# Seven products inside each of seven: a second level of Strassen's scheme in the second feed-forward layer of six groups

## The chip, the cores and the metric

The kernel runs on one core of one Trainium2 chip. The metric is the device time of one execution in microseconds (us); the figure for the kernel before is the median of three runs, 1125.85 us, with runs from 1123.66 to 1127.17. Each core has TensorE (matrix products, in the profile PE; its weight loads PEld), VectorE (DVE), ScalarE (ACT) and GpSimd (POOL) for elementwise work, and SyncE (SP), which issues the transfers. SBUF is the on-chip memory of 128 partitions, PSUM holds the sums that TensorE makes, and DRAM is off the chip.

## The reference

A linear attention is followed by a Fourier mixing of tokens and columns, a normalization, and two feed-forward layers with a residual, all in fp32. Cut to what matters:

```python
# attention on (batch 8, heads 8, seq 576, head_dim 64): softmax of q over head_dim, of k over seq
kv = np.einsum('bhsd,bhse->bhde', k_s, v)
x = np.einsum('bhsd,bhde->bhse', q_s, kv)          # turned to (8, 576, 512)
# mixing and feed-forward
X = np.fft.fft(np.fft.fft(x, axis=1), axis=2)
u = x + np.real(X)
mu = np.mean(u, axis=-1, keepdims=True)
var = np.mean((u - mu) ** 2, axis=-1, keepdims=True)
un = (u - mu) / np.sqrt(var + 1e-06)
ch = np.maximum(un @ w_ch1, 0.0) @ w_ch2           # w_ch1 512 x 2048, w_ch2 2048 x 512
return u + ch
```

## The kernel before

The 8 x 576 tokens are nine groups of 512: eight are made of 512 tokens of one batch each, and one of the 64 that each batch leaves over. The first group uses plain products while the weights arrive. The other eight, numbered by `at` from 1 to 8, use Strassen's seven-product scheme (in Winograd's form) once in each layer: a product of 2 x 2 blocks is made of seven block products instead of eight, at the price of sums of blocks before and after. The sums of the weights' blocks are made once on the chip, put in DRAM (`w1s`, `w2s`) and streamed back for each group through a ring of four SBUF buffers of 1 MB (`load`, `used`). For h, the output of the first layer, the sums are made by GpSimd (`a_side`). `ORDER` is the order of the seven products; `A_AT` and `B_AT` say in which of seven slots the left and the right operand of each product stand. Slots 0, 1 and 3 and, at first, 2 hold raw blocks of h; slots 2, 4, 5 and 6 hold sums after `a_side`. Two matmuls that share one PSUM bank (`ba`, `bb`, `bc`) leave 128 x 512 results.

In `down`, the second layer, each product is 16 matmuls of 128 x 128 weights with 256 columns. While TensorE goes through them, the attention, transform and normalization of the next groups are merged between them as side steps (`merged(down, two + norm)`). The functions that the change touches, empty lines left out:

```python
A_AT = {1: 0, 2: 1, 3: 6, 4: 3, 5: 4, 6: 5, 7: 2}
B_AT = {1: 0, 2: 2, 3: 3, 4: 6, 5: 4, 6: 5, 7: 1}
WA_AT = {1: 0, 2: 1, 3: 6, 4: 2, 5: 4, 6: 5, 7: 3}
WB_AT = {1: 0, 2: 1, 3: 2, 4: 6, 5: 4, 6: 5, 7: 3}
WORDS_AT = [*range(8), 8, 9, 10, *range(3, 8), 0, 1, 2, 8, 9, 10, 4, 5, 6, 7, 8, 11, 12, 7, 13, 8]
LATE_WORDS = (27, 28, 30)
ORDER = (1, 6, 5, 7, 2, 4, 3)
# ... (cut)
    def a_side(self, at, to, e1, e2):
        e1.tensor_tensor(out=to(4), in0=at(2), in1=at(3), op=ALU.add)
        e1.tensor_tensor(out=to(2), in0=at(0), in1=at(2), op=ALU.subtract)
        e2.tensor_tensor(out=to(5), in0=to(4), in1=at(0), op=ALU.subtract)
        e2.tensor_tensor(out=to(6), in0=at(1), in1=to(5), op=ALU.subtract)
# ... (cut)
    def load(self, n):
        g, i = divmod(n, NP + 7)
        if g > B:
            return
        k = n % 4
        w = self.big[:, k * NP * HD:(k + 1) * NP * HD].rearrange("p (a n) -> p a n", n=HD)
        if i < NP:
            self.nc.sync.dma_start(w[:, 0:7, :], self.w1s[i][:])
        else:
            self.nc.sync.dma_start(w, self.w2s[WB_AT[ORDER[i - NP]]])
        self.stream[n] = w
    def hpairs(self, p, n):
        a = 2 * NF * D + p * 7 * HD if p < NP // 2 else NF * D + (p - NP // 2) * 7 * HD
        return self.big[:, a:a + n * 7 * HD].rearrange("p (a s n) -> p a s n", s=7, n=HD)
# ... (cut)
    def strassen(self, product, out, early=lambda *a: None):
        nc, V = self.nc, self.nc.vector
        box = {}
        def bank(n):
            box[n] = self.ps.tile([P, 2, HD], F32, tag=n, name=n)
        def temp(n):
            box[n] = self.work.tile([P, 2, HD], F32, tag=n, name=n, bufs=1)
            return box[n][:]
        def m1():
            nc.scalar.copy(temp("s1"), box["ba"][:])
            early(2, 1, box["s1"])
        def m6():
            V.tensor_tensor(out=temp("u2"), in0=box["bb"][:], in1=box["s1"][:], op=ALU.add)
            early(1, 2, box["u2"])
        def m7():
            V.tensor_tensor(out=temp("u3"), in0=box["bb"][:], in1=box["s1"][:], op=ALU.add)
            early(2, 2, box["u3"])
            out[2, 2](box["bc"], box["u3"])
        ends = {1: m1, 6: m6, 7: m7, 2: lambda: out[1, 1](box["ba"], None),
                4: lambda: out[2, 1](box["bb"], box["s1"]), 3: lambda: out[1, 2](box["bc"], box["u2"])}
        at = {1: "ba", 2: "ba", 6: "bb", 7: "bb", 4: "bb", 5: "bc", 3: "bc"}
        steps = []
        for m in ORDER:
            first = m in (1, 6, 5)
            parts = product(m, lambda m=m: box[at[m]], first, m in (2, 4, 3))
            begin = [lambda m=m: bank(at[m])] if first else []
            end = [ends[m]] if m in ends else []
            steps.append(begin + parts + end)
        return steps
    def up(self, at, unT):
        nc, V = self.nc, self.nc.vector
        steps = []
        for j in range(NP // 2):
            pairs = (2 * j, 2 * j + 1)
            hp = lambda i, h=self.hpairs(2 * j, 2): h[:, :, i, :]
            def product(m, bank, first, last, pairs=pairs):
                def run(i):
                    w = self.stream[15 * at + pairs[i]]
                    for k in range(2):
                        nc.tensor.matmul(bank()[:, i, :], lhsT=w[:, WA_AT[m], k * P:(k + 1) * P],
                                         rhs=unT[:, B_AT[m], k, :], start=first and i == 0 and k == 0,
                                         stop=k == 1,
                                         skip_group_check=True)
                return [lambda i=i: run(i) for i in range(2)]
            def c11(bank, _, hp=hp):
                nc.scalar.activation(hp(0), bank[:], ACT.Relu)
            def other(i, hp=hp):
                def run(bank, u):
                    V.tensor_tensor(out=hp(i), in0=bank[:], in1=u[:], op=ALU.add)
                    nc.scalar.activation(hp(i), hp(i), ACT.Relu)
                    if i == 2:
                        self.a_side(hp, hp, nc.gpsimd, nc.gpsimd)
                return run
            job = self.strassen(product, {(1, 1): c11, (2, 1): other(1), (2, 2): other(3), (1, 2): other(2)})
            steps.append([s for m in job for s in m] + [lambda p=p: self.used(15 * at + p) for p in pairs])
        return steps
    def used(self, n):
        self.stream.pop(n)
        self.load(n + 4)
    def down(self, g, at):
        nc, V = self.nc, self.nc.vector
        h = [self.hpairs(p, 1)[:, 0] for p in range(NP)]
        last = at == B
        def product(m, bank, first, final):
            n = 15 * at + NP + ORDER.index(m)
            order = (1, 0) if last and m == 3 else (0, 1)
            def run(i, q):
                w = self.stream[n]
                for p in range(4 * q, 4 * q + 4):
                    nc.tensor.matmul(bank()[:, i, :], lhsT=h[p][:, A_AT[m], i * P:(i + 1) * P], rhs=w[:, p, :],
                                     start=first and i == 0 and p == 0, stop=p == NP - 1,
                                     skip_group_check=True)
                if (i, q) == (order[1], 1):
                    self.used(n)
                if last and m in (4, 3) and q == 1:
                    sums(m == 4, m != 4, bank(), i)
            return [lambda i=i, q=q: run(i, q) for i in order for q in range(2)]
        def early(i, j, t):
            u, d = i - 1 if (i, j) != (1, 2) else 0, j - 1
            x = self.xs[g, u][:, :, d * HD:(d + 1) * HD]
            nc.gpsimd.tensor_tensor(out=x, in0=x, in1=t[:], op=ALU.add)
        def sums(u, d, bank, i):
            x = self.xs[g, u][:, i, d * HD:(d + 1) * HD]
            V.tensor_tensor(out=x, in0=bank[:, i, :], in1=x, op=ALU.add)
# ... (cut: out, which adds the four results from PSUM into x with VectorE, L1020)
# ... (cut)
        jobs, down = blk.up(order, nexts.pop(g)), blk.down(g, order)
        merged(flat(jobs), one)
        merged(down, two + (norm(groups[order + 1]) if order < B else []))
```

The instructions of these helpers stand in the profile under these lines: L957 is the matmul of `up`, L995 that of `down`; L362 to L365 are `a_side`; L369 to L372 are `b_side` on the normalized input; L921, L925 and L929 are `m1`, `m6` and `m7` of `strassen`; L964, L968 and L969 finish h; L1007 and L1020 add into x. L418 and L420 are the loads of the stream.

## Time and profile before

| what | value |
|---|---|
| time, median of three | 1125.85 us (1123.66 to 1127.17) |
| span of the profiled execution | 1126.2 us |
| mean granted TensorE clock | 0.991 |
| moved by DMA | 193.79 MB, mean 172 GB/s |
| first layers of the groups 1 to 8 (L957), stretch of one | 60 to 63 us (48 to 50 in the last two) |
| second layers of the groups 1 to 8 (L995), stretch of one | 57 to 61 us (49 in the last two) |

How to read it: a row of the groups gives the line, the engine, the operation, the tiles out<-in with their shapes, the count, then busy time in us and the mean duration of one in ns, then the engine's idle time just before these instructions and what ended it. A matmul in fp32 is recorded as two instructions, so the counts of L957 and L995 are twice the number of matmuls in the code. A timeline row gives the start and the length of a run of like instructions in us. A stretch row gives, for a window of time, the busy time and count of each engine.

### The profile page before, as it was taken

How to read it: one execution, taken by the hardware profiler on the slowest of the kernel's cores; microseconds unless marked ns; L12 is line 12 of the kernel's file. 1: busy time of each engine (PE TensorE's matmuls, PEld its weight loads, DVE VectorE, ACT ScalarE, POOL GpSimd, SP SyncE). 2: the span in 40 equal slices, each digit the busy share in tenths (PEclk: the TensorE clock that was granted, in tenths of full speed). 3: DMA queues.
4: the chain of work that ended last, by engine and by line, in shares of the span. 5: the costliest groups of instructions: out<-in, count | busy, mean ns of one | idle time of the engine just before them, and what ended most of it. 6: DMA issues, size and time to landing. Idle time of an engine off the chain costs nothing.

```text
span 1126.2 us, 14461 instructions
## 1 busy us (share of the span) xinstructions
PE 1088.4 (97%) x5376; PEld 909.9 (81%) x5376; DVE 545.4 (48%) x1121; ACT 403.5 (36%) x973; POOL 331.9 (29%) x303
## 2 busy tenths in 40 slices
PE   5789989999999999999999999999999999999997
PEld 4644545887888888898889888888889888888886
DVE  6694796368423734375344643583444352103301
ACT  6695434255233513362325332542334152201200
POOL 1065571235013510324024402251034203402320
PEclk8899999999999999999999999999999999999999
DMA  9555786464246534554356435642453444434451
GB/s 305 176 190 188 259 291 220 145 224 166 98 150 211 195 127 145 195 172 171 125 173 221 150 106 190 198 185 108 147 191 150 144 144 144 187 141 157 152 187 56
DMA packets 92581, 193.79 MB, mean 172 GB/s; under 512 B 23120, under 2 KB 59728, under 8 KB 85344
## 3 DMA queue, kind: packets, MB, share of 16 engines
q1 hardware_dynamic: 90712, 191.82, 49.9%
q10 hardware_dynamic: 1800, 1.05, 0.3%
q8 instruction: 43, 0.70, 0.2%
q14 instruction: 26, 0.21, 0.1%
HBM read 168.72 MB, written 28.31 MB: 175 GB/s over the span
## 4 chain that ended last, share of the span: by engine, by line
PE 81%; POOL 3%; issue 2%; ACT 1%; DVE 1%; ACTq 0%; POOLq 0%
PE bb L957 14%; PE bb L995 14%; PE bc L995 10%; PE ba L957 9%; PE bc L957 9%; PE ba L995 9%; PE acc L568 2%; PE acc L658 2%; PE bc L896 2%; PE acc L752 1%; PE acc L776 1%; PE acc L755 1%; PE tr L857 1%; PE tr L554 1%; PE tr L623 1%
## 5 line engine op out<-in xcount | busy, mean ns | idle before, releaser
L957 PE MATMUL bb<-unT,big 128*128 128x256 f32 x768 | 187.4, 381 | 0.2 <-DVE u L925 0.2
L995 PE MATMUL bb<-big 128*128 128x256 f32 x768 | 172.1, 379 | 0.0
L957 PEld LDWEIGHTS bb<-unT,big 128*128 128x128 f32 x768 | 142.8, 190 | 23.9 <-DVE u L925 3.0
L995 PEld LDWEIGHTS bb<-big 128*128 128x128 f32 x768 | 145.4, 190 | 20.3
L362 POOL TENSOR_TENSOR big<-big 128x512 f32<-128x512 f32 (+1 forms) x38 | 46.2, 1216 | 307.6 <-ACT big L969 306.8
L969 ACT ACTIVATE big<-big 128x512 f32<-128x512 f32 x96 | 60.3, 629 | 182.7 <-DVE big L968 182.2
L957 PE MATMUL bc<-unT,big 128*128 128x256 f32 x512 | 125.4, 379 | 0.0
L957 PE MATMUL ba<-unT,big 128*128 128x256 f32 x512 | 123.6, 379 | 0.2 <-ACT unT L861 0.2
L995 PE MATMUL bc<-big 128*128 128x256 f32 x512 | 116.0, 379 | 0.5 <-DVE x L1012 0.5
L995 PE MATMUL ba<-big 128*128 128x256 f32 x512 | 114.8, 379 | 0.0
L929 DVE TENSOR_TENSOR u<-bb,s 128x512 f32<-128x512 f32 x40 | 27.6, 691 | 173.1 <-PE bb L995 116.1
L995 PEld LDWEIGHTS bc<-big 128*128 128x128 f32 x512 | 96.1, 190 | 14.3 <-DVE x L1012 0.9
L995 PEld LDWEIGHTS ba<-big 128*128 128x128 f32 x512 | 95.7, 190 | 12.1
L957 PEld LDWEIGHTS bc<-unT,big 128*128 128x128 f32 x512 | 95.1, 190 | 12.6
L957 PEld LDWEIGHTS ba<-unT,big 128*128 128x128 f32 x512 | 95.1, 190 | 12.2 <-ACT unT L861 0.5
L370 POOL TENSOR_TENSOR unT<-unT 128x512 f32<-128x512 f32 x8 | 14.2, 1772 | 179.8 <-DVE unT L369 179.8
L607 ACT ACTIVATE q<-q,qm 128x64 f32<-128x64 f32 x240 | 61.6, 338 | 6.8 <-DVE qm L605 6.6
L925 DVE TENSOR_TENSOR u<-bb,s 128x512 f32<-128x512 f32 x40 | 27.5, 688 | 71.7 <-PE bb L957 38.7
L968 DVE TENSOR_TENSOR big<-bc,u 128x512 f32<-128x512 f32 x64 | 44.1, 689 | 22.8 <-PE bc L957 21.7
L1007 POOL TENSOR_TENSOR x<-x,u 128x512 f32<-128x512 f32 x14 | 17.7, 1267 | 118.8 <-DVE u L929 99.0
L861 ACT COPY unT<-tr 128x512 f32<-128x512 f32 x36 | 20.7, 585 | 79.9 <-PE tr L857 79.3
L968 DVE TENSOR_TENSOR big<-bb,s 128x512 f32<-128x512 f32 x32 | 22.1, 691 | 56.1 <-PE bb L957 56.1
(254 smaller groups left out, 1640.8 us busy)
## 6 DMA issues: line engine op xcount, KB each, us to landing
big<-w1s SPq DMA_DIRECT2D x64, 896.0 KB
big<-w2s SPq DMA_DIRECT2D x56, 1024.0 KB
big<-in_w_dram SPq DMA_DIRECT2D x21, 512.0 KB
q<-in_q_dram SPq DMA_DIRECT2D x27, 256.0 KB
k<-in_kT_dram SPq DMA_DIRECT2D x24, 288.0 KB
v<-in_v_dram SPq DMA_DIRECT2D x24, 256.0 KB
words<-in_w_dram SPq DMA_DIRECT2D x8, 512.0 KB
mirror<-x SPq DMA_DIRECT2D x14, 256.0 KB
```

Of the source, the lines that this page charges most:

```text
L362: e1.tensor_tensor(out=to(4), in0=at(2), in1=at(3), op=ALU.add)
L568: nc.tensor.matmul(pk, lhsT=ks[:, c, :], rhs=v[:, c, :], start=(c == 0), stop=(c == NC - 1))
L607: nc.scalar.activation(heads[:, h, :], heads[:, h, :], ACT.Exp, bias=m[:, h:h + 1])
L658: nc.tensor.matmul(px[:, r * P:(r + 1) * P], lhsT=qT[:, r, :], rhs=self.kvr[b % 2][:, r, :], start=True, stop=True)
L861: nc.scalar.copy(unT[:, u:u + 3:2, :, cols], pt[:].rearrange("p (a k) t -> p a k t", a=2))
L896: nc.tensor.matmul(po[:], lhsT=h[:, f, i * P:(i + 1) * P], rhs=self.w2sb[:, f, :], start=(f == 0), stop=(f == NF - 1))
L925: V.tensor_tensor(out=temp("u2"), in0=box["bb"][:], in1=box["s1"][:], op=ALU.add)
L929: V.tensor_tensor(out=temp("u3"), in0=box["bb"][:], in1=box["s1"][:], op=ALU.add)
L957: nc.tensor.matmul(bank()[:, i, :], lhsT=w[:, WA_AT[m], k * P:(k + 1) * P], rhs=unT[:, B_AT[m], k, :], start=first and i == 0 and k == 0, ...
L968: V.tensor_tensor(out=hp(i), in0=bank[:], in1=u[:], op=ALU.add)
L969: nc.scalar.activation(hp(i), hp(i), ACT.Relu)
L995: nc.tensor.matmul(bank()[:, i, :], lhsT=h[p][:, A_AT[m], i * P:(i + 1) * P], rhs=w[:, p, :], start=first and i == 0 and p == 0, stop=p == ...
```

## The change

The second layer of the groups 2 to 7 (`deep`) is made in two levels of the same scheme: each of the seven block products is itself split into 2 x 2 blocks and made of seven smaller ones. A first-level product had 16 matmuls of 256 columns; now its seven parts have four matmuls of 128 columns each, 28 in all, over half the columns. It is meant to cut the multiplications of this layer by one eighth.

For this the weights need second-level sums. They do not change from group to group, so group 1, which still uses one level, makes them as its first-level sums pass through (`deepen`: two operations on VectorE and two on GpSimd for each product), and writes all 49 weight blocks to DRAM (`w2d`). The deep groups stream `w2d` in place of `w2s`, four blocks (1 MB) per buffer.

The second-level sums of h are made in each deep group (`a_steps`: for each first-level product two on VectorE and two on GpSimd). The seven first-level products are done in four units, `UNITS`: product 1 alone, then three pairs; the two of a pair share the PSUM banks and the evacuations. Within a unit the 14 or 7 small products go in `ORDER`, and the sums for the next unit are spread between them. The result of a first-level product is put together in its own dead slot 0 block and then added into x by GpSimd (`into`), where the scheme before added three results with GpSimd and four from PSUM with VectorE. Because the second level needs the first half and the second half of h's columns apart, `up` now handles the pairs of blocks j and j + 4 together (`PAIRS`).

The core of the diff, empty lines left out:

```diff
+UNITS = ((1,), (2, 4), (7, 6), (5, 3))
+DEEP = [(m, n) for unit in UNITS for n in ORDER for m in unit]
+PAIRS = [(j + NP // 2, j) for j in range(NP // 2)]
...
+        self.plan, self.base = [], {}
+        for at in range(1, B + 1):
+            self.base[at] = len(self.plan)
+            self.plan += [self.w1s[p][:].rearrange("p a n -> p (a n)") for pair in PAIRS for p in pair]
+            if self.deep(at):
+                for i in range(0, len(DEEP), 4):
+                    self.plan.append(self.w2d[:, i:min(i + 4, len(DEEP)), :].rearrange("p a n -> p (a n)"))
+            else:
+                self.plan += [self.w2s[WB_AT[m]].rearrange("p a n -> p (a n)") for m in ORDER]
         self.big = c.tile([P, 3 * NF * D], F32, name="big")
...
+    def deep(self, at):
+        return 1 < at < B
...
+    def deepen(self, m, w, t):
+        nc = self.nc
+        at = lambda i: w[:, i // 2 * 4:i // 2 * 4 + 4, i % 2 * P:i % 2 * P + P]
+        to = lambda i: t[(1, 4, 5, 6).index(i)]
+        e1, e2 = nc.vector, nc.gpsimd
+        e1.tensor_tensor(out=to(4), in0=at(1), in1=at(0), op=ALU.subtract)
+        e1.tensor_tensor(out=to(1), in0=at(3), in1=at(1), op=ALU.subtract)
+        e2.tensor_tensor(out=to(5), in0=at(3), in1=to(4), op=ALU.subtract)
+        e2.tensor_tensor(out=to(6), in0=at(2), in1=to(5), op=ALU.subtract)
+        for n in (1, 2, 3, 5, 7, 6, 4):
+            i = B_AT[n]
+            to_dram = self.w2d[:, DEEP.index((m, n)), :].rearrange("p (f n) -> p f n", n=P)
+            nc.sync.dma_start(to_dram, to(i) if i in (1, 4, 5, 6) else at(i))
+    def deep_down(self, g, at, unT):
+        nc, V, G = self.nc, self.nc.vector, self.nc.gpsimd
+        base = self.base[at] + NP
+        un = lambda i: unT[:, i].rearrange("p k n -> p (k n)").rearrange("p (f n) -> p f n", n=P)
+        dead = lambda m: [self.hblock(A_AT[m], a, b) for a, b in ((0, 1), (1, 0), (1, 1))]
+        temps = {1: [self.gap(i) for i in range(3)], 4: [un(i) for i in range(3)], 2: [un(i) for i in range(3, 6)],
+                 6: dead(1), 7: [self.gap(i) for i in range(3)], 5: dead(4), 3: dead(2)}
+        result = {m: self.hblock(A_AT[m], 0, 0) for m in A_AT}
+        tile = lambda m: result[m].rearrange("p (c e) n -> p c e n", c=2)
+        def own(m):
+            def at(i):
+                return temps[m][i - 4] if i > 3 else self.hblock(A_AT[m], i // 2, i % 2)
+            return at
+        def a_steps(unit):
+            steps = []
+            for m in unit:
+                to = own(m)
+                for o, x, y, e, op in ((4, 2, 3, V, ALU.add), (2, 0, 2, V, ALU.subtract), (5, 4, 0, G, ALU.subtract),
+                                       (6, 1, 5, G, ALU.subtract)):
+                    steps.append(lambda to=to, o=o, x=x, y=y, e=e, op=op: e.tensor_tensor(out=to(o), in0=to(x), in1=to(y),
+                                                                                          op=op))
+            return steps
+        def into(u, d, m):
+            x = self.xs[g, u][:, :, d * HD:(d + 1) * HD].rearrange("p c (e n) -> p c e n", n=P)
+            G.tensor_tensor(out=x, in0=x, in1=tile(m), op=ALU.add)
...
+        after = {(1,): [lambda: into(0, 0, 1)],
+                 (2, 4): [lambda: into(1, 0, 4), lambda: into(0, 0, 2)],
+                 (7, 6): [lambda: sums(6, 1), lambda: into(0, 1, 6), lambda: sums(7, 6), lambda: into(1, 0, 7),
+                          lambda: into(1, 1, 7)],
+                 (5, 3): [lambda: into(1, 1, 5), lambda: store(1), lambda: into(0, 1, 5), lambda: into(0, 1, 3),
+                          lambda: store(0)]}
+        place = {1: "ba", 2: "ba", 6: "bb", 7: "bb", 4: "bb", 5: "bc", 3: "bc"}
+        def unit_steps(unit):
+            k, box = len(unit), {}
+            def bank(n):
+                box[n] = self.ps.tile([P, 2, P], F32, tag=n, name=n)
+            def temp(n):
+                box[n] = self.work.tile([P, 2, P], F32, tag=n, name=n, bufs=1)
+                return box[n][:, 0:k]
+            def product(n):
+                def run(i):
+                    m, to = unit[i], own(unit[i])
+                    q = DEEP.index((m, n))
+                    w = self.stream[base + q // 4]
+                    first = n in (1, 6, 5)
+                    if first and i == 0:
+                        bank(place[n])
+                    for f in range(4):
+                        r = q % 4 * 4 + f
+                        nc.tensor.matmul(box[place[n]][:, i, :], lhsT=to(A_AT[n])[:, f, :],
+                                         rhs=w[:, r // 2, r % 2 * P:r % 2 * P + P], start=first and i == 0 and f == 0,
+                                         stop=f == 3, skip_group_check=True)
+                    if q % 4 == 3 or q == len(DEEP) - 1:
+                        self.used(base + q // 4)
+                return [lambda i=i: run(i) for i in range(k)]
+            def plus(out, n, t):
+                V.tensor_tensor(out=out, in0=box[n][:, 0:k], in1=t[:, 0:k], op=ALU.add)
+            def block(j, n, t=None):
+                slots = [A_AT[m] for m in unit]
+                out = self.hpairs(j)[:, slots[0]:slots[-1] + 1:max(slots[-1] - slots[0], 1), 0:P]
+                if t is None:
+                    nc.scalar.copy(out, box[n][:, 0:k])
+                else:
+                    plus(out, n, box[t])
+            ends = {1: lambda: nc.scalar.copy(temp("s1"), box["ba"][:, 0:k]),
+                    6: lambda: plus(temp("u2"), "bb", box["s1"]),
+                    7: lambda: (plus(temp("u3"), "bb", box["s1"]), block(3, "bc", "u3")),
+                    2: lambda: block(0, "ba"), 4: lambda: block(2, "bb", "s1"), 3: lambda: block(1, "bc", "u2")}
+            steps = []
+            for n in ORDER:
+                steps += product(n) + ([ends[n]] if n in ends else [])
+            return steps
+        steps = a_steps(UNITS[0])
+        for i, unit in enumerate(UNITS):
+            ahead = a_steps(UNITS[i + 1]) if i + 1 < len(UNITS) else []
+            steps += mixed(unit_steps(unit), ahead) + after[unit]
+        return steps
...
+    def down(self, g, at, unT):
+        if self.deep(at):
+            return self.deep_down(g, at, unT)
         nc, V = self.nc, self.nc.vector
-        h = [self.hpairs(p, 1)[:, 0] for p in range(NP)]
+        h = [self.hpairs(p) for p in range(NP)]
         last = at == B
         def product(m, bank, first, final):
-            n = 15 * at + NP + ORDER.index(m)
+            n = self.base[at] + NP + ORDER.index(m)
+            k = ORDER.index(m)
+            spare = [self.hblock(A_AT[ORDER[k - 1]], a, b) for a in range(2) for b in range(2)]
             order = (1, 0) if last and m == 3 else (0, 1)
             def run(i, q):
                 w = self.stream[n]
+                if at == 1 and (i, q) == (order[0], 0):
+                    self.deepen(m, w, spare if k % 2 else [self.gap(i) for i in range(4)])
                 for p in range(4 * q, 4 * q + 4):
                     nc.tensor.matmul(bank()[:, i, :], lhsT=h[p][:, A_AT[m], i * P:(i + 1) * P], rhs=w[:, p, :],
                                      start=first and i == 0 and p == 0, stop=p == NP - 1,
...
```

## The prediction

> **What bounds the kernel now.** I read the page's engine totals first, then the groups of instructions by line, then stretches of one group's cycle, and last the timelines.
>
> ```profile
> PE 1088.4 (97%) x5376; PEld 909.9 (81%) x5376; DVE 545.4 (48%) x1121; ACT 403.5 (36%) x973; POOL 331.9 (29%) x303
> ...
> L995 PE MATMUL bb<-big 128*128 128x256 f32 x768 | 172.1, 379 | 0.0
> ```
>
> TensorE is busy for 97% of the span, and the largest group of the second layer (L995) has no idle time ahead of it. So every microsecond of matmul streaming taken out is worth up to a microsecond, as long as no wait comes in its place. What a matmul streams is read from starts in TensorE's timeline, not from the mean duration of 379 ns, which overlaps its neighbours:
>
> ```profile
> 384.15 7.07 PE L995 MATMUL ba<-big 128*128 128x256 f32 x32
> 391.06 7.07 PE L995 MATMUL bb<-big 128*128 128x256 f32 x32
> ...
> 818.03 1.28 PE L568 MATMUL acc<-v,ks 128*128 128x128 f32 x10
> 819.15 0.60 PE L554 MATMUL tr<-ident,k 128*128 128x128 f32 x4
> ```
>
> 32 records of 256 columns last from 384.15 to 391.06: 216 ns each. Ten records of 128 columns, each with weights of its own, last from 818.03 to 819.15: 112 ns each. One fp32 matmul leaves two records, so it costs 432 ns at 256 columns and 224 ns at 128. The L995 rows have 2 x 896 records: 8 groups x 7 products x 16 matmuls. One second layer is 112 x 0.432 = 48.4 us. Its whole stretch, here that of group 2, is 58.3 us, since some 10 us of the next group's transform and transposes stand between the products. Split where the helpers change their load:
>
> ```profile
> 384.10:400.00 15.90, 15.90 (x79) 14.03 (x79) 15.04 (x32) 4.80 (x13) 8.87 (x7) 1.00 0.55 201
> 400.00:442.40 42.40, 42.40 (x225) 37.74 (x224) 11.72 (x35) 10.93 (x26) 2.53 (x2) 1.00 0.36 128
> ```
>
> The columns are length, then busy time of PE, weight loads, VectorE, ScalarE and GpSimd, the clock, the DMA share and GB/s. In the first 16 us VectorE is full (15.0) and GpSimd more than half full (8.9); later both are nearly free. TensorE does not notice now, because one product of 16 matmuls lasts 6.9 us and covers any late helper.
>
> **What the Trainium skill says.** "SBUF — State Buffer", section "Who interferes with whom", states that a VectorE instruction with two SBUF inputs contends with a GpSimd instruction that reads SBUF, and that the second to issue fully blocks. The trace agrees:
>
> ```profile
> 386.04 1.76 DVE L699 TENSOR_TENSOR eo<-x 128x512 f32<-128x512 f32 x1
> ...
> 388.46 1.75 DVE L699 TENSOR_TENSOR eo<-x 128x512 f32<-128x512 f32 x1
> ```
> ```profile
> 385.88 1.37 POOL L362 TENSOR_TENSOR big<-big 128x512 f32<-128x512 f32 x1 [2.34 <-ACT big L969]
> 387.21 1.18 POOL L714 TENSOR_TENSOR eo<-eo 128x257 f32<-128x257 f32 x1
> 388.35 1.31 POOL L363 TENSOR_TENSOR big<-big 128x512 f32<-128x512 f32 x1
> ```
>
> The same kind of VectorE operation takes 0.69 us alone (L369), and here 1.76, ending half a microsecond after GpSimd's operation does. "TensorE: Matmul & The Clock Gate", section "Step-by-step: what each phase is for", says that the next weights load while the running matmul streams, and its section "LDWEIGHTS (loading the stationary operand)" gives P/1.2 ns for P columns, an estimate of 107 ns for 128. At 216 ns per record that hides with room to spare, at 112 ns only just; L568 shows that it still does over ten in a row. No run here shows a hundred in a row. On the transfers I rely on the trace alone.
>
> **The change part by part.**
>
> *Streaming.* A deep second layer has 49 products of 4 matmuls of 128 columns: 196 x 0.224 = 43.9 us against 48.4, so 4.5 us less. Six groups: -27.0 us. If nothing else moved, 1125.9 - 27.0 = 1098.9 us.
>
> *VectorE, per deep group.* Added: 14 combinations of h (two for each first-level product) x 0.69 (L369) = 9.7 us; evacuations, five in each unit, three units at 0.69 and the single one at 0.42 (the 128x256 size of L791): 12.4. Removed: six at 0.69 = 4.1. Net +18, so 26.8 becomes about 45 of some 54 us.
>
> *GpSimd, per deep group.* Added: 14 combinations and 11 additions into x or between results, 25 operations of 1.27 us (L362, L1007); removed: three additions. Net 22 x 1.27 = +28, so 11.4 becomes about 39. The sum of both is what matters because of the lock: GpSimd about 35 us net of its own blocking, VectorE's new combinations 14 x 0.55, and the old folds and mixes with two SBUF inputs some 12: 55 us of lock in a 54 us stretch. It fits on average only since the additions into x may run late.
>
> *ScalarE.* Eight copies in place of one, +3.6 us on 15.7: no matter.
>
> *Transfers.* A deep layer streams 49 x 256 KB = 12.8 MB in place of 7.3; the one-time writing is another 12.8. Total 193.8 + 6 x 5.5 + 12.8 = 240 MB, 214 GB/s over the span. In the deep stretch a piece of 1 MB serves 16 matmuls, 3.6 us of TensorE, or 4.4 with what lies between. Packet times between 384 and 389 us show 420 KB per us while a load runs, and a lone 1 MB load is over in 4 us including its ramp. With four buffers it has three pieces (11 us) of notice. I take it as hidden.
>
> *Where waits come in.* First, the start of the stretch. The first unit needs raw blocks of h alone, and its combinations can run before the last first-layer product ends, so its second product should hardly wait. The second unit's product 6 comes some 8 us in. Ahead of it GpSimd has four old combinations (5.1 us), part of the transform's six (6.4 us before), and two new ones (2.5), each alternating with a blocked VectorE operation of 0.55. That is 11 to 13 us of work: I count 2 us of wait for each of the five groups with a transform, 1 for the sixth: 11 us. Second, the PSUM banks: product 7 may not enter its bank before product 6 was read, with only product 5 between, 0.9 us in the single unit and 1.8 in pairs, against 0.73 for a free VectorE and up to 2 for a blocked one. I count 0.7 us per group: 4 us. Third, GpSimd's last three additions meet the combinations of the next group's normalized input; product 6 of the next first layer waits 0.4 us for these now (2.6 over 7), and each may be blocked once: 0.8 per group, 5 us. Fourth, the group that makes the combinations writes 12.8 MB beside 8.9 MB in 61 us, 356 GB/s, close to the 420 seen: 2 us. Together 22 us.
>
> 1098.9 + 22 = 1121 us.
>
> **The rivals.** (a) *The lock becomes the bound.* If the list of helpers keeps the transform ahead of the new combinations, the second unit starts 6 to 9 us late and each deep stretch gets longer than now: 6 more us in five groups, 1121 + 30 = 1151. For it: VectorE's 15.0 of 15.9 us. Against it: the stretch after 400 us, where both helpers are idle, and the order of units, which begins with blocks that need no first-level sums. (b) *Everything is hidden.* Only bank waits and the writing group remain: about 1105. For it: the present kernel already keeps TensorE without gaps under VectorE's full load. Against it: a product now lasts 0.9 or 1.8 us, not 6.9. (c) *Weights or transfers bind.* If 128-column matmuls went at 123 ns (the busy time of L568's weight loads, 29.6 us over 240), a deep layer would be 48.2 us and the whole gain gone: 1147 with the waits. If the loads fell behind, TensorE would stand at the first matmul of every fourth product; this would be at its worst in the deep stretches, which ask for 12.8 of 54 us x 420 KB = 23 MB.
>
> **Range and chances.** The streaming gain is nearly certain, the 22 us of waits are not: I can see from 2 to 50. So the range is 1101 to 1150. More than 2% faster means under 1103.3 us, that is waits of under 5 us in all: 0.13. More than 2% slower means above 1148.4, rival (a) in full: 0.19. The rest, 0.68.
>
> **What would show it right or wrong.** Records of the deep matmuls at 112 ns from start to start, 2352 in all; TensorE's idle time in deep stretches at their beginning, ended by GpSimd's combinations of h, and small idle times ended by VectorE's evacuations; VectorE's h combinations near 1.2 us in the mean in place of 0.69; the stretch of the sixth deep group, without a transform, shortened the most. Idle time ended by a weights transfer would make it wrong, as would a pitch near 123 ns, or deep stretches without any idle time.

## The result: 7.1% slower, and the profile after

The changed kernel takes 1206.03 us (median of four runs, 1203.46 to 1209.93) against 1126.51 us of the kernel before, measured beside it on the same chip: a ratio of 1.0713, with a 95% interval from 1.0677 to 1.0749. The prediction was 1121 us, its range ended at 1150.

The rows of the page of the changed kernel that answer to those shown of before. Its first layer is now L986, the deep second layer L1091, the second layer of groups 1 and 8 L1143. The first-level sums of h are L377 to L380 (before L362 to L365), the second-level sums L1048, the evacuations of the deep layer L1099 (VectorE) and L1105, L1109 (ScalarE), the additions into x L1054.

```profile
PE 1088.4 (90%) x6384; PEld 938.5 (78%) x6384; DVE 685.7 (57%) x1303; ACT 416.9 (35%) x1015; POOL 550.0 (46%) x449
...
PE 66%; DVE 11%; POOL 7%; issue 2%; ACT 2%; DMA 1%; SPq 0%; POOLq 0%; DVEq 0%; ACTq 0%
...
L1091 PE MATMUL bb<-big 128*128 128x128 f32 x912 | 124.3, 290 | 53.0 <-DVE big L1048 30.2
...
L1048 POOL TENSOR_TENSOR big<-big 128x512 f32<-128x512 f32 x60 | 91.7, 1537 | 38.0 <-DVE big L1048 34.2
...
L1048 DVE TENSOR_TENSOR big<-big 128x512 f32<-128x512 f32 x72 | 76.0, 1075 | 13.8 <-POOL big L379 6.7
...
L1099 DVE TENSOR_TENSOR u<-bb,s 128x256 f32<-128x256 f32 (+1 forms) x48 | 18.4, 384 | 69.2 <-PE bb L1091 68.8
```

The row of engine shares is that of the chain of work that ended last. Before, it was:

```profile
PE 81%; POOL 3%; issue 2%; ACT 1%; DVE 1%; ACTq 0%; POOLq 0%
```

TensorE was 97% busy and is 90% busy. In the chain its share fell from 81% to 66%, and VectorE and GpSimd took 18% of it where they had 4%. The row of L1091 now has 53.0 us of idle time ahead of it; the row of L995 that stood there before had none. The mean of one second-level sum in these rows is 1075 ns on VectorE and 1537 ns on GpSimd.

What TensorE stood still for, as the view of the line L1091 lists it (us, times). It adds up both of TensorE's queues, matmuls and weight loads, which mostly stand still together, so about half of each figure is time:

```profile
  DVE big L1048: 61.3, 8
  DVE u L1099: 44.2, 16
  DVE big L997: 14.5, 6
  POOL big L1048: 3.4, 2
  ACT s L1109: 3.2, 5
```

A good half of the waiting is for sums of h (L1048), over a third for evacuations (L1099, L1109), the rest for the finish of h itself (L997). No transfer is in the list.

The stretches from the first to the last matmul of a layer, out of the two traces (us):

| | before | after |
|---|---|---|
| group 1, first and second layer | 63.2, 60.5 | 69.3, 72.0 |
| second layers of groups 2 to 6 | 58.1, 57.0, 58.1, 57.1, 58.1 | 65.7, 67.6, 68.2, 68.6, 66.5 |
| second layer of group 7 | 49.4 | 56.9 |
| first layers of groups 2 to 6 | 61.0, 62.4, 61.0, 62.3, 61.0 | 62.7, 64.1, 62.4, 64.3, 62.4 |
| first layers of groups 7 and 8 | 50.1, 48.5 | 51.2, 48.5 |

So of the 81.9 us between the two profiled spans (1126.2 and 1208.1) the six deep stretches have 55.7, group 1 has 17.6, the other first layers have 9.3. Streaming did become shorter: between the starts of one deep matmul record and the next lie 112 ns in the median, over 2352 records. From the starts of all matmuls, a nominal pitch for each shape and what goes beyond it, I get about 27 us less of streaming, 91 us more of waits and 19 us more (about 10 before, 29 after) lost to matmuls that run at half their rate.

Group 2's deep stretch, cut where the helpers' load changes, with the columns of the prediction (length; busy time of PE, weight loads, VectorE, ScalarE, GpSimd; clock; DMA share; GB/s):

```profile
403.08:425.00 21.92, 13.03 (x100) 12.54 (x99) 19.81 (x33) 6.22 (x22) 18.66 (x15) 0.84 0.47 179
425.00:469.00 44.00, 43.03 (x372) 42.29 (x371) 28.81 (x67) 14.83 (x38) 22.48 (x16) 1.00 0.55 197
```

Nearly all the harm is in the first 22 us: VectorE is busy for 19.8 and GpSimd for 18.7 of them, TensorE does 13.0 us of work, and its clock is 0.84. Behind them TensorE is nearly as busy as before. The other deep groups are alike: by the starts of their matmuls the six lose about 67 us to waits and 14 to half the rate in the first 22 us of each, and 2 us later. TensorE's timeline of that place in group 2:

```profile
405.76 1.06 PE L1091 MATMUL ba<-big 128*128 128x128 f32 x8
414.44 2.08 PE L1091 MATMUL bb<-big 128*128 128x128 f32 x8 [7.62 <-DVE u L1099]
```

VectorE's and GpSimd's in the same place:

```profile
405.34 1.76 DVE L728 TENSOR_TENSOR eo<-x 128x512 f32<-128x512 f32 x1
...
408.29 1.75 DVE L728 TENSOR_TENSOR eo<-x 128x512 f32<-128x512 f32 x1
...
412.45 1.73 DVE L1048 TENSOR_TENSOR big<-big 128x512 f32<-128x512 f32 x1 [1.15 <-POOL big L379]
414.11 0.28 DVE L1099 TENSOR_TENSOR u<-bb,s 128x128 f32<-128x128 f32 x1
```
```profile
406.51 1.71 POOL L377 TENSOR_TENSOR big<-big 128x512 f32<-128x512 f32 x1
...
409.45 1.71 POOL L378 TENSOR_TENSOR big<-big 128x512 f32<-128x512 f32 x1
411.12 1.30 POOL L379 TENSOR_TENSOR big<-big 128x512 f32<-128x512 f32 x1
```

Read backwards from 414.44. The matmuls that start there are product 7 of the first unit (product 2 ran ahead of it at 405.76). Product 7 goes into the bank of product 6, and TensorE waits for the evacuation of that bank, 0.28 us of work (L1099). Product 6 was done near 405. But VectorE takes its work in order, and ahead of the evacuation stand two folds of the transform (L728), two operations of the attention (L709 and L710, 1.35 us each) and a sum of h that waits for GpSimd's first-level sum L379. Each of the folds and the sum takes 1.7 us where the sum alone takes 0.69, since it alternates with an operation of GpSimd. That sum is also the left operand of product 7. In groups 3, 4, 5 and 7 the longest wait of TensorE, 6.59 to 8.68 us, is at this same product and ends with the sum itself.

### The profile page after: what moved, and what is told of

It reads as the page before. It is cut to its first block, busy times and chain, and to the rows that moved or that the text cites. A ratio compares the mean times of both kernels' runs of the same rounds, so it can differ in the third digit from the quotient of the medians.

```text
span 1208.1 us, 17183 instructions
## 1 busy us (share of the span) xinstructions
PE 1088.4 (90%) x6384; PEld 938.5 (78%) x6384; DVE 685.7 (57%) x1303; ACT 416.9 (35%) x1015; POOL 550.0 (46%) x449
## 3 DMA queue, kind: packets, MB, share of 16 engines
q1 hardware_dynamic: 115624, 237.70, 57.1%
## 4 chain that ended last, share of the span: by engine, by line
PE 66%; DVE 11%; POOL 7%; issue 2%; ACT 2%; DMA 1%; SPq 0%; POOLq 0%; DVEq 0%; ACTq 0%
PE bb L986 13%; PE bb L1091 9%; PE bc L986 8%; PE ba L986 8%; PE bc L1091 6%; PE ba L1091 5%; PE acc L597 2%; PE bc L1143 2%; PE acc L687 2%; DVE big L1048 2%; PE bb L1143 2%; POOL unT L1048 2%; PE bc L925 1%; POOL eo L728 1%; PE tr L886 1%
## 5 line engine op out<-in xcount | busy, mean ns | idle before, releaser
L986 PE MATMUL bb<-unT,big 128*128 128x256 f32 x768 | 188.2, 382 | 4.6 <-DVE unT L386 4.6
L1091 PE MATMUL bb<-big 128*128 128x128 f32 x912 | 124.3, 290 | 53.0 <-DVE big L1048 30.2
L986 PEld LDWEIGHTS bb<-unT,big 128*128 128x128 f32 x768 | 143.7, 191 | 26.2 <-DVE unT L386 7.4
L377 POOL TENSOR_TENSOR big<-big 128x512 f32<-128x512 f32 (+1 forms) x38 | 47.4, 1246 | 252.3 <-ACT big L998 251.5
L1091 PEld LDWEIGHTS bb<-big 128*128 128x128 f32 x912 | 116.4, 204 | 56.7 <-DVE big L1048 31.1
L986 PE MATMUL bc<-unT,big 128*128 128x256 f32 x512 | 125.6, 381 | 2.2 <-DVE unT L384 2.2
L986 PE MATMUL ba<-unT,big 128*128 128x256 f32 x512 | 122.7, 379 | 0.2 <-ACT unT L890 0.2
L1048 POOL TENSOR_TENSOR big<-big 128x512 f32<-128x512 f32 x60 | 91.7, 1537 | 38.0 <-DVE big L1048 34.2
L986 PEld LDWEIGHTS bc<-unT,big 128*128 128x128 f32 x512 | 95.3, 191 | 15.9 <-PE ba L986 4.0
L986 PEld LDWEIGHTS ba<-unT,big 128*128 128x128 f32 x512 | 95.3, 190 | 12.3 <-ACT unT L890 0.5
L1091 PE MATMUL ba<-big 128*128 128x128 f32 x672 | 90.4, 286 | 1.3 <-ACT s L1109 1.3
L1054 POOL TENSOR_TENSOR x<-x,big 128x512 f32<-128x512 f32 x45 | 65.4, 1469 | 55.8 <-DVE big L1099 39.7
L1091 PEld LDWEIGHTS ba<-big 128*128 128x128 f32 x672 | 86.2, 202 | 3.4 <-ACT s L1109 1.9
L1048 DVE TENSOR_TENSOR big<-big 128x512 f32<-128x512 f32 x72 | 76.0, 1075 | 13.8 <-POOL big L379 6.7
L958 DVE TENSOR_TENSOR u<-bb,s 128x512 f32<-128x512 f32 x34 | 23.5, 691 | 86.4 <-PE bb L986 65.7
L1091 PE MATMUL bc<-big 128*128 128x128 f32 x480 | 63.1, 284 | 7.0 <-DVE big L997 7.0
L1091 PEld LDWEIGHTS bc<-big 128*128 128x128 f32 x480 | 59.7, 200 | 7.5 <-DVE big L997 7.5
L997 DVE TENSOR_TENSOR big<-bc,u 128x512 f32<-128x512 f32 x64 | 44.1, 689 | 25.5 <-PE bc L986 24.1
L1099 DVE TENSOR_TENSOR u<-bb,s 128x256 f32<-128x256 f32 (+1 forms) x48 | 18.4, 384 | 69.2 <-PE bb L1091 68.8
L954 DVE TENSOR_TENSOR u<-bb,s 128x512 f32<-128x512 f32 x34 | 23.4, 690 | 58.6 <-PE bb L986 44.0
```

Source lines behind the costliest of these rows:

```text
L1048: steps.append(lambda to=to, o=o, x=x, y=y, e=e, op=op: e.tensor_tensor(out=to(o), in0=to(x), in1=to(y), op=op))
L1054: G.tensor_tensor(out=x, in0=x, in1=tile(m), op=ALU.add)
L1091: nc.tensor.matmul(box[place[n]][:, i, :], lhsT=to(A_AT[n])[:, f, :], rhs=w[:, r // 2, r % 2 * P:r % 2 * P + P], start=first and i == 0 an ...
```

## The experiments

Two theories fit the picture.

**W, write after read.** The sum `(2, 0, 2, V)` of the first two units, one of the second-level sums that the prediction calls combinations, is written in place, into a slot that `a_side` of the last pair still has to read. So VectorE cannot go on until GpSimd has done its first-level sums. The prediction said that the first unit "needs raw blocks of h alone"; it reads raw blocks alone, but it writes one too.

**L, the lock and the order.** VectorE's operations with two operands in SBUF and GpSimd's operations hold each other up, so that a fold or a sum that VectorE does alone in 0.69 us takes up to 1.76; what the two share is called the port in the texts below. And VectorE's queue is in order, so that short evacuations stand behind long blocked operations.

The other terms of the sum get runs of their own: the one-time writing in group 1, the additions at the start of the next first layer. The kernels are variants of the changed kernel. Those that differ from it in several ways are built up step by step, and each section says on what.

### Only the in-place write taken away

```diff
-   (4, 2, 3, V, ALU.add), (2, 0, 2, V, ALU.subtract), ...
+   (4, 2, 3, V, ALU.add), (7, 0, 2, V, ALU.subtract), ...
...
-   lhsT=to(A_AT[n])[:, f, :]
+   lhsT=to(7 if n == 7 else A_AT[n])[:, f, :]
```

In the first two units slot 7 is memory of its own; in the others it is slot 2 as before.

> Edit: the sum that replaces a raw block of h (second operation of each product) goes to memory of its own in units 1 and 2, with the same operations on the same engines. Theory W (write after read): in the changed kernel these in-place writes must wait until GpSimd's first-level sums of the last pair have read the same blocks, VectorE stands there in order, and the read of the PSUM bank behind it holds TensorE for 7 to 9 us in each deep group. W expects that idle time to go, deep stretches of 58 to 60 us in place of 57 to 68.6, and about 1160 us (1148 to 1172). Rival L (volume under the shared port): what holds TensorE is the sum of VectorE's and GpSimd's work; L expects the wait to stay, 1195 us or more.

1204.69 us, ratio to before 1.0704 [1.0676, 1.0732]. W as the sole cause falls: the difference to 1206.03 is within the noise, and the deep stretches are 64.8, 67.6, 67.7, 67.5, 66.5 and 55.1 us. The wait has only moved. TensorE's and VectorE's timelines of group 2 in this run:

```profile
417.89 1.44 PE L1091 MATMUL bb<-big 128*128 128x128 f32 x5 [4.15 <-DVE u L1099]
```
```profile
411.95 3.42 DVE L728 TENSOR_TENSOR eo<-x 128x512 f32<-128x512 f32 x2
415.29 2.34 DVE L734 TENSOR_TENSOR eo<-eo 128x255 f32<-128x255 f32 x2
417.55 0.28 DVE L1099 TENSOR_TENSOR u<-bb,s 128x128 f32<-128x128 f32 x1
```

No sum of h stands between the folds and the evacuation now, and still the 0.28 us of it come 5.6 us after the folds began.

### Only the last pair's first-level sums on VectorE

```diff
-   self.a_side(hp, hp, nc.gpsimd, nc.gpsimd)
+   self.a_side(hp, hp, *(2 * [V if self.deep(at) and j == 3 else nc.gpsimd]))
```

> Edit: in deep groups the four first-level sums of the last pair of h run on VectorE (0.69 us each) and not on GpSimd (1.27 to 1.7 each, behind other work). W expects the in-place writes to be released 3 to 4 us earlier: 1180 to 1190 us. L expects nothing or a loss, since VectorE gets 2.8 us more work in its fullest stretch and both engines' sum hardly falls: 1203 to 1215.

1198.02 us, 1.0638 [1.0613, 1.0662], between the two. Group 7, whose stretch has no transform, gains 4.6 us (56.9 to 52.3), so there the wait for the first-level sums is a good part. The five stretches with a transform gain 7.7 us together.

### Only the second-level sums on VectorE, alone and out of place

```diff
-   (5, 4, 0, G, ALU.subtract), (6, 1, 5, G, ALU.subtract)
+   (5, 4, 0, V, ALU.subtract), (6, 1, 5, V, ALU.subtract)
```

> Edit: the second-level sums of h all run on VectorE; GpSimd keeps the first-level sums and the additions into x. GpSimd loses 14 operations of 1.54 us per deep group, VectorE gets 14 of 0.69. If the port shared by the two is what stretches VectorE's queue (L), its sums fall from 1.08 us in the mean to about 0.75 and the time to 1180 to 1192 us. If VectorE's own amount of work is the bound, the time rises to 1210 or more.

1182.05 us, 1.0513 [1.049, 1.0537]: 24 us less, though VectorE gets 14 more operations per group. VectorE's second-level sums, now 132 in that row of the profile, take 749 ns in the mean where 72 took 1075. That is in L's range. The run does not part two causes: the sums no longer block each other, and the moved ones also run on the engine that needs 0.69 us alone for what GpSimd needs 1.27 for. With the out-of-place write as well:

> Edit: the second-level sums of h all on VectorE and the replacing sums of units 1 and 2 out of place; the last pair's first-level sums stay on GpSimd. In the run with the sums on VectorE alone, product 7 of unit 1 still waits 6.4 us, the last 4 of them after the bank was read, for an in-place sum that follows GpSimd's reading of the block. If W holds once the port is relieved, out of place is now worth 3 to 5 us per group, where it was worth nothing alone: 1153 to 1165. If out of place is worth nothing in any setting, 1180 again.

1175.07 us, 1.0436 [1.0415, 1.0458]: the out-of-place write, worth 1 us alone, is worth 7 here.

### All three edits

> Edit: three together: all second-level sums of h on VectorE, the last pair's first-level sums on VectorE, and the replacing sums of units 1 and 2 out of place. At the start of a deep stretch GpSimd then has the transform's folds alone, and nothing waits for a block to be read. If the waits are those of the shared port and of VectorE's order (L), the deep stretches come to about 58 us and the time to 1160 to 1172. If the gains of the parts do not add up because VectorE is full, it stays above 1185.

1153.80 us, 1.0254 [1.0233, 1.0276], better than expected. Alone the three parts brought 1, 8 and 24 us, together 52: each alone leaves a wait that ends where the next one begins. In particular, the last pair's sums bring 8 us on the changed kernel and 21 when the other two edits are in. The deep stretches are 61.1, 58.3, 57.3, 58.3, 57.1 and 45.8 us.

### No sums of h at all

This run leaves out both the second-level sums of h and, as the run without weight sums below, those of the weights; the products take raw blocks in their place.

```diff
-   for m in unit:          # a_steps
+   for m in ():
-   lhsT=to(A_AT[n])[:, f, :]
+   lhsT=to(A_AT[n] % 4)[:, f, :]
```

> Edit: no second-level sums at all, neither of h nor of the weights; the products read raw blocks and the deep groups stream first-level weights of the same size (a time only). This leaves the streaming, the evacuations and the additions into x. If the sums of h and what they hold up are the whole loss, deep stretches come to 53.8 us (45 for group 7) and the time to 1099 to 1108. If the short products or the PSUM banks cost by themselves, as the bank waits of the prediction would, stretches stay at 57 or more and the time at 1118 or more.

1151.33 us, 1.0236 [1.0202, 1.0269], which misses the first range by far; the second case came, stretches of 57 or more. Group 7's stretch is 45.7 us, close to the 43.9 of pure streaming, so nothing else stood in its way. The stretches with a transform stay at 60.5, 64.3, 59.0, 64.2 and 60.8. The six together come to 354.5 us, against 393.5 in the changed kernel and 310.8 for those of before less 27 us of streaming. So about 39 us of the deep stretches' excess go with the sums of h, and 44 us remain without any. Three quarters of that lie in the first 22 us of the stretches, here in TensorE's and VectorE's timelines of group 2:

```profile
393.38 2.08 PE L1091 MATMUL bb<-big 128*128 128x128 f32 x8 [3.17 <-DVE u L1099]
```
```profile
389.10 1.75 DVE L728 TENSOR_TENSOR eo<-x 128x512 f32<-128x512 f32 x1
390.77 2.34 DVE L734 TENSOR_TENSOR eo<-eo 128x255 f32<-128x255 f32 x2
393.04 0.28 DVE L1099 TENSOR_TENSOR u<-bb,s 128x128 f32<-128x128 f32 x1
```

The evacuation again stands behind folds. These were in the kernel before too, at the same length (1.76 us for a fold). There a product lasted 6.9 us and nobody waited. The last quarter, some 11 us, comes late in the stretches, where in groups 3 and 5 an evacuation stands behind the next group's mixing and normalization (waits of 2.88 and 2.89 us).

The run above, with all sums on VectorE, has shorter deep stretches in sum (337.9 us) than this one with none: it takes the last pair's first-level sums off GpSimd too. VectorE's folds of x (L728) take 1363 ns in the mean here and 857 there. Of the difference of 17 us about 10 lie in the first 22 us of the stretches, as if unblocked work on VectorE cost less than a smaller amount beside GpSimd. The other 7 are the late waits. The two runs differ in the places of the side steps as well, so this comparison hints at the lock but does not prove it.

### The transform's folds placed later in the list

```diff
-   merged(down, two + (norm(...) if order < B else []))
+   merged(down, [lambda: None] * (10 if blk.deep(order) and two else 0) + two + (norm(...) if order < B else []))
```

> Edit: in deep groups the transform of the next group is merged in later, so that its folds begin in unit 2 and not at the start; no operation is added or moved to another engine. L expects the wait at the start to shrink by about 6 us in the five groups that have a transform: 1173 to 1183, with group 7 (none) unchanged at 57 us. If only the in-place writes behind the last pair's sums count (W), GpSimd still reaches these sums after the new ones, the gain stays under 2 us per group: 1196 or more.

1264.38 us, 1.1237 [1.1213, 1.1261]: L missed, and W's "1196 or more" had no loss of 58 us in view. The deep stretches with a transform grew to between 75.7 and 79.1 us. Waits such as 3.90 us for an evacuation behind folds and mixes now come late in the stretch, beside 7.03 us at its start. Later is not better here.

### The folds on VectorE too, and free slots in group 1

On the version with all three edits; GpSimd's half of the folds goes to VectorE.

```diff
-   e, op = ((V if b == 0 else G), ALU.add) if i < 2 else (V, ALU.subtract)
+   e, op = ((V if b != 1 else G), ALU.add) if i < 2 else (V, ALU.subtract)
...
```

> Edit: the run with all sums on VectorE and out of place, and in addition the transform's folds on VectorE only (but for the second batch). GpSimd then does nothing at the start of a deep stretch. VectorE gets some 4 us more work of its own there and loses every wait for the port. If the port is what keeps the evacuations late in VectorE's queue (L), deep stretches fall to 55 or 56 us and the time to 1138 to 1146. If it is the sheer length of VectorE's queue, the time stays at 1150 or rises.

1149.04 us, 1.0213 [1.0175, 1.0252]: 5 us less, below what L expected. Its interval overlaps that of the version without the edit, so the gain isn't certain. The deep stretches did not fall to 55 or 56 us: they are 337.2 us in sum, where they were 337.9. So with the second-level and the last first-level sums already off GpSimd, taking the folds off it as well brought nothing there, as the other case of the expectation says. Then, on top of it, the weights' sums of group 1 into slots of h that are dead, from the second product on:

```diff
-   self.deepen(m, w, spare if k % 2 else [self.gap(i) for i in range(4)])
+   self.deepen(m, w, spare if k else [self.gap(i) for i in range(4)])
```

> Edit: as the run before, and group 1 puts its second-level weight sums into dead slots of h for every product but the first, not into one small buffer for every other. VectorE then waits in order for TensorE and no longer for transfers that still read that buffer. The run without the writes was worth 8 us; if half of that is this waiting, 4 to 6 us less than the run before; if the transfers' own load is the cost, no change.

1138.99 us, 1.0123 [1.0098, 1.0148]: 10 us less, twice the expected. The second layer of group 1 goes from 67.8 to 57.9 us.

### Group 1 by itself

On the changed kernel, first without the writes of the weights' sums: the deep groups then stream first-level blocks of the same size in their place, so their products are not those of the reference. Then without the sums as well.

```diff
-   nc.sync.dma_start(to_dram, to(i) if i in (1, 4, 5, 6) else at(i))
+   pass
```

> Edit: group 1 still makes the second-level sums of the weights but does not write them to DRAM; the deep groups stream first-level weights of the same size (results differ, so this is a time only). If the 12.8 MB of writing, and VectorE waiting in order for buffers that a write has not read yet, make group 1 slow, its two layers fall from 141 to about 125 us and the time to about 1190. If it is the sums on VectorE and GpSimd that hold up the transform and the attention, no more than 6 us go: 1200.

1198.08 us, 1.0635 [1.0613, 1.0657]: nearer to the second case. Group 1's two layers take 135.6 us, far from the expected 125.

> Edit: group 1 neither makes nor writes second-level weights; the deep groups stream first-level weights of the same size (a time only). Both views of group 1 expect its layers back at 124 us, as in the kernel before, and 1187 to 1191 us; the difference to the run without the writes alone is what the sums cost. The deep stretches should stay at 57 to 68 us: 1188 if so, less if the writes also slowed later groups.

1188.16 us, 1.0551 [1.0536, 1.0567], as expected: group 1's layers are back at 63.2 and 60.8 us and the deep stretches are unchanged. Group 1 thus costs 18 us, 8 for the writes and 10 for the sums. VectorE's timeline of the changed kernel shows what a write does to a sum: the four temporary slots are used by turns, and the sums wait until the transfer has read them.

```profile
295.88 0.69 DVE L1017 TENSOR_TENSOR big<-big 128x512 f32<-128x512 f32 x1 [3.98 <-DMA w2d<-big]
```

Last, the 5 us wait in group 1's first layer. The sums of the first product's weights run early, since those weights lie ready. On the version of 1138.99 us they were moved behind that product:

```diff
-   if at == 1 and (i, q) == (order[0], 0):
+   if at == 1 and k and (i, q) == (order[0], 0):
...
...
-   self.used(n)
+   (at != 1 or k) or self.deepen(m, w, ...), self.used(n)       # ...: the product's own dead slots
```

> The version with everything on VectorE, free slots in group 1 and the folds moved (1138.99 us), with one more edit: the weights' sums for the first product of group 1's second layer are made after that product instead of before it, into its own dead slots. What is left of group 1's cost is a 5 us wait at the end of its first layer, where the transposes of q wait for a VectorE operation behind those sums. If these sums, run early because their weights lie ready, cause it, group 1's first layer goes from 69.1 to 63-65 us and the time falls by 3 to 6 us: 1133-1136. If the wait has another cause (the first layer's own helpers), the time stays within 1.5 us of 1139.

1136.91 us, 1.0087 [1.0071, 1.0103]. The first layer goes from 69.1 to 65.4 us, so the early sums cause most of what was left there. The medians differ by only 2.1 us, less than expected, and the two intervals overlap.

### The additions at the start of the next first layer

GpSimd's last three additions into x (L1054) run while the next normalized input is combined. Three runs gave them out after the first two steps of the next first layer, the third together with the later sums of group 1 and with the transform's folds as single steps of the list. In that place the additions collide with the next x, probably since it takes over the same buffer, so these three kernels do not compute the reference and their times count for little.

> The same base (1138.99 us) with the last three additions into x of a deep group issued after the first two steps of the next group's first layer, in place of right before it. The third wait term of the prediction (5 us for six groups) said that they block the combinations of the normalized input there. If so, the first layers after a deep group with a transform shrink by 1 to 2 us each and the total falls by 6 to 11 us: 1128-1133. If the first layers wait for something else at their start, under 3 us comes back: 1136-1140.

1146.82 us, 1.0183 [1.0153, 1.0214].

> The changed kernel itself (1206 us) with only the last three additions of each deep group issued after the first two steps of the next first layer. This measures the third wait term on the changed kernel: the prediction's size is 5 us in all, the lengths of the first layers say 9. So 1196-1202 if the additions are the cause; within 2 us of 1206 if not.

1216.21 us, 1.0798 [1.0777, 1.0819].

> Both of these edits, and the transform's folds given out as single operations, spread over the deep stretch, in place of blocks of four to eight: the theory that evacuations stand behind whole blocks in VectorE's queue says that the five deep groups with a transform (57.4-59.6 us on this base) come to 54-56, so 13 to 20 us less in them, and with the two edits 1106-1122 us, for the first time below the kernel before (1126). If only the amount of VectorE's work counts and not its grouping, the deep groups stay above 57 and the time is 1125-1133.

1168.48 us, 1.0372 [1.0355, 1.0389]. All three are slower than their base, against every expectation: the waits at the start went, but the first layers grew by up to 5 us elsewhere, and with the single folds TensorE waited 3.47 us near the end of group 4's deep stretch. Then the additions were given out right behind the combinations, ahead of the next first layer:

```diff
-   (5, 3): [lambda: into(1, 1, 5), lambda: store(1), lambda: into(0, 1, 5), lambda: into(0, 1, 3), lambda: store(0)]
+   (5, 3): []          # kept as a list, tail
...
+   [s() for s in tail]
    merged(flat(jobs), one)
```

> The changed kernel (1206 us) with only the last three additions into x of each deep group given out after the combinations of the next normalized input, but ahead of all of the next first layer. Two runs before gave them out two steps later, where they collide with the next x, so the values were lost and their times are not those of this kernel. If the additions cause the 9 us that the first layers after deep groups lost, 1196-1202; if the time only moves elsewhere, as those two runs hint (the first layers there grew by 2 to 3 us), 1204-1212.

1194.27 us, 1.0614 [1.0586, 1.0641]: 12 us less on the changed kernel, just beyond the expected range. The five first layers that follow groups 2 to 6 go from 64.1, 62.4, 64.3, 62.4 and 51.2 to 62.2, 60.5, 62.5, 60.5 and 49.4. With the same edit on the version of 1136.91 us:

> The version with all sums and folds on VectorE, free slots and the first product's weight sums later (1136.9 us), with the same edit. If the additions cause the start waits: first layers after deep groups 1 to 2 us shorter each, 1128-1132. If the time only moves: 1135-1142.

1126.98 us, ratio 1.0005 [0.9995, 1.0015], just under the expected range: as fast as the kernel before, and 79 us faster than the changed kernel. The start of a first layer before this edit (in the run of 1138.99 us) in TensorE's timeline, and GpSimd's:

```profile
574.18 0.67 PE L986 MATMUL bc<-unT,big 128*128 128x256 f32 x2 [0.43 <-DVE unT L384]
575.76 1.99 PE L986 MATMUL bb<-unT,big 128*128 128x256 f32 x8 [0.91 <-DVE unT L386]
```
```profile
572.22 4.62 POOL L1054 TENSOR_TENSOR x<-x,big 128x512 f32<-128x512 f32 x3 [7.11 <-DVE big L1099]
576.80 1.72 POOL L385 TENSOR_TENSOR unT<-unT 128x512 f32<-128x512 f32 x1
```

With the edit, the same two timelines:

```profile
568.15 1.89 PE L986 MATMUL bb<-unT,big 128*128 128x256 f32 x8
569.88 1.89 PE L986 MATMUL bc<-unT,big 128*128 128x256 f32 x8
```
```profile
565.33 1.27 POOL L385 TENSOR_TENSOR unT<-unT 128x512 f32<-128x512 f32 x1 [5.96 <-DVE unT L384]
568.35 3.85 POOL L1054 TENSOR_TENSOR x<-x,big 128x512 f32<-128x512 f32 x3 [1.75 <-DVE big L1099]
```

GpSimd's own combination (L385) stood behind three additions of another group; now it goes first and TensorE doesn't wait.

### What is left: grouping or amount of the folds

> As the run before, with the transform's folds as single operations over the first quarter of the deep stretch only, so that the rest of the list is not pushed back. The run with single folds spread by the list lost 4 us at the end of each deep stretch, where the next group's normalization came late, while its waits at the start fell from about 3.3 to 1.3 us. If grouping is what makes evacuations wait, deep groups with a transform come to 55-57 us (57.4-59.6 on the base) and the time is 6 to 12 us under the run before; if the amount of work alone counts, it is within 3 us of it.

1129.42 us, 1.0022 [1.0009, 1.0035]: not faster than the run before. The deep stretches with a transform, 58.6, 58.4, 58.6, 58.8 and 58.9 us there, are 59.7, 58.9, 59.2, 59.2 and 57.5 here. Folds given out singly don't help. Each of these stretches still has some 5 us over 53.2 (57.7 before in the mean, less 4.5 of streaming). The traces point to the amount of VectorE's work, though no run takes any of it away. In the first 22 us of group 2's stretch in the run of 1138.99 us, in the columns of above, VectorE is busy all the time and GpSimd hardly at all; three folds take 1.89 us together, where one took 1.75 in the changed kernel:

```profile
388.24:410.14 21.90, 19.09 (x158) 18.11 (x157) 21.90 (x53) 4.08 (x13) 2.19 (x1) 1.00 0.67 240
```
```profile
392.81 1.89 DVE L728 TENSOR_TENSOR eo<-x 128x512 f32<-128x512 f32 x3
```

So the blocking is gone there, and an evacuation still stands behind whatever VectorE has ahead of it, with waits of 0.53 and 1.58 us for TensorE.

## Why the prediction was wrong

*Streaming* was right: 112 ns from start to start over 2352 records, about 27 us less against 27.0. Where nothing stood in the way (group 7 in the run with no sums) a deep layer took 45.7 us.

*VectorE's and GpSimd's added work* came out near the prediction. Group 2's deep stretch has 48.6 us of VectorE where it had 26.8, so +21.9 against +18 predicted; GpSimd has 41.1 where it had 11.4, so +29.7 against +28. For VectorE that is partly luck, since two errors cancel. I put its 20 evacuations per group at 0.69 and 0.42 us, 12.4 in all; they take 0.385 in the mean, 7.7. And I put its 14 sums at 0.69 us, 9.7 in all; blocked, they take 1.064 in the mean, 14.9. The row of 72 sums shown above has 1075 ns against "near 1.2". Rival (c) did not come: no transfer of weights ended a wait in a deep stretch.

*The waits*, 22 us in the sum, were the failure. They came to 91 us, and 19 us of slower clock beside them. By term:

- **The start of the stretch, and the PSUM banks** (11 and 4 us predicted). The deep stretches grew by 55.7 us in spite of 27 us less streaming, so they lost 83 us where 15 were counted, of which about 68 are waits and 15 half the rate. The first term rests on the step "its combinations can run before the last first-layer product ends, so its second product should hardly wait". That step failed. In group 2 products 6 and 5 did start at once, but the combination that product 7 reads overwrites a block that GpSimd's first-level sums still need; it began 9.4 us into the stretch, and product 7 waited 7.62 us. Over the six deep groups the waits at this product make 45 us. The in-place write was a part of it, though only together with the rest, since without it TensorE waits for evacuations instead: 1 us alone, 7 with the sums on VectorE. The bank term failed in its size: I gave an evacuation "0.73 for a free VectorE and up to 2 for a blocked one", as if one operation were ahead of it. The evacuation itself takes 0.28 to 0.42 us, but in the run out of place four operations, 5.6 us, stand right ahead of one at the end of an in-order queue. Without a single second-level sum 44 of the 83 us remained; with three edits that take sums off GpSimd and the write out of place, 56 of them went (393.5 to 337.9 us).
- **The additions at the next first layer** (5 us): mechanism right, size off. They cost 12 us of time on the changed kernel, 9 of them in the five first layers, which shrank by 1.8 to 1.9 us each where I had put 0.8. I had each combination blocked once, while GpSimd's own combination came behind all three additions.
- **The writing group** (2 us): 18 us. I compared GB/s, and the transfers were not the limit: with the same writes, but from dead slots, the second layer of group 1 went from 67.8 to 57.9 us. On the changed kernel the sums cost 10 us and the writes 8, the latter in part since sums waited for slots that a write still read.
- **The clock**, 19 us, was not counted at all.

The sign that the sixth deep group, without a transform, would be shortened the most failed too: it grew from 49.4 to 56.9 us.

Of the rivals (a) was nearest: "the second unit starts 6 to 9 us late" is close to the 7.62 us, though the wait stands inside the first unit. Its cause, a transform ahead of the sums, is not the whole of it: group 7 has no transform, and TensorE waited 7.17 us there. Its price, 30 us more, was still too low. The prediction had counted the lock as an average, "it fits on average only since the additions into x may run late": 55 us of lock in a 54 us stretch. But the work comes in the first 22 us, and there TensorE has products of 0.9 us, which hide nothing.

## What to carry to other kernels

Where a product is cut to an eighth of its length, a helper's operation of 1.7 us that was free beside a product of 6.9 us becomes a wait beside one of 0.9. Before such a change, ask for each short evacuation what stands ahead of it in its engine's queue, blocked by whom, and count in-place writes as waits for all readers. And before spreading work over two engines, ask whether they block each other: here moving 14 operations per group from GpSimd to the busier VectorE took 24 us away.

## What the runs showed of the chip that was not expected

TensorE is mostly slower after a wait of about three microseconds or more. In the profile of the changed kernel, eight records took 2.08 us after the wait of 7.62, against 1.06 before it; in the run with no sums, 2.08 after 3.17 (at 393.38). After waits of 1.89 and 2.25 us (the run out of place) the rate was full. The border is not sharp: in the run with no sums eight records took 1.16 us, the full rate, after a wait of 3.16 us (at 647.16), and 2.08 after one of only 2.65 (at 895.18). "TensorE: Matmul & The Clock Gate", section "What's actually happening" in the Trainium skill, gives half the clock by default and after an idle window of about 3.4 us, and full after about as much of work. It says that these windows run freely, which fits waits of 3 us that end either way. By the matmuls' starts the half rate costs about 29 us in the changed kernel, 10 in the one before and 13 in the best version.

The blocking reached further than I had thought. A sum of h that takes 0.69 us alone took 1.7 beside GpSimd, as the skill's "SBUF — State Buffer", section "Who interferes with whom", leads one to expect. But I had counted GpSimd's operations at 1.27 us throughout, and they grew as well: its second-level sums take 1.50 us in the mean of all 84, and L377 and L378 took 1.71 us each in the timeline above. The same section allows for it, as it says that the order of issue decides which of the two is held up.
